# An attention block's output projection moved inside its core, and the last products' operands loaded into freed ring buffers

## The chip, the cores and the metric

One NeuronCore of one Trainium2 chip. The metric is device time in microseconds (us), the median of several executions. Single totals are compared with care, and stages are compared in the traces.

## The reference, cut to what matters

Two attention blocks, A (linear attention) and B (16 query heads over one shared key/value head), each on 2048 tokens of width 448, forward and backward. Only B matters here:

```python
q = (x @ wq).reshape(B, S, 16, 28).transpose(0, 2, 1, 3)     # B_x is (1, 2048, 448)
k, v = x @ wk, x @ wv                                        # one head of 28
p = softmax(einsum("bhqd,bkd->bhqk", q, k) * 28 ** -0.5)
o = einsum("bhqk,bkd->bhqd", p, v)
out = o.transpose(0, 2, 1, 3).reshape(B, S, 448) @ wo        # "the output projection"
# ... and the gradients of x, wq, wk, wv and wo
```

## The kernel before

After block A come 540 "units" `u`, the core. A unit computes scores and exponentials for a slice of 256 keys, the gradient rows of the unit 16 earlier, and more at longer lags. Eight units are a block (one pair of heads, 256 queries); 64 units are a query block of 256 queries. The order of instructions in the core is the program's, engine by engine (no scheduler moves them). Of the names below, eT holds exponentials and eN their transposes; oTs is a block's output as it is copied out of PSUM, onat the normalised output with tokens on the partitions, on_d its copy in DRAM, and oTq (new in the change) the transpose of onat that the output projection reads. gwo, gwq, gwk and gwv are gradients of weights, dx that of x, dq that of the queries.

```python
psS = tile_pool(name="psS", bufs=3, PSUM)    # "sps": scores and small transposes
psD = tile_pool(name="psD", bufs=2, PSUM)    # "dps"
oq, dv_acc, dk_acc = ...                     # one PSUM bank each: all 8 banks are taken
pe_, pn_, pd_ = ...                          # rings eT (10 buffers), eN (11), dsT (4)
...
for u in range(NU + 28):                     # NU = 512
    if u == 14 or u % 64 == 0 and 0 < u < NU:
        # qX: 16 loads of 64 KB on the SP queue; first read at unit u + 28
    # scores -> sps, exp on ScalarE -> eT; at odd u: eN <- DMA transpose of eT (SP queue)
    # gradient rows -> dps; VectorE and ScalarE + GpSimd -> dsT
    e = u - 9
    if e >= 0 and e % 8 == 0 and e // 8 < NB:
        # two transposes of oTs into an sps buffer; VectorE normalises them into onat
        if pair == 7:                        # end of a query block: u % 64 == 1
            nc.sync.dma_start(on_d[...], onat)          # 256 KB to DRAM
    # dk_acc, oq and dv_acc matmuls
    if 0 <= v < NU and v % 8 == 7:           # v = u - 1, so u % 8 == 0
        nc.vector.tensor_copy(out=oTs[v // 8], in_=oq[0:64, 0:256])
# ---- [cut] the tail: new pools, everything loaded here
nc.sync.dma_start(onat_B, on_d)              # 2 MB
load_nat(gb, grad_out); load_nat(xb, B_x)    # 4 x 448 KB each
for g in range(4):
    nc.sync.dma_start_transpose(oT[g], on_d[:, g * P:(g + 1) * P])
for g in range(4):
    nc.sync.dma_start_transpose(dqn[:, :, ...], qT_B[g])
# gwo = onat_B^T gb (64 matmuls); then 16 x (dx: 5 matmuls; output projection: 4 matmuls);
# then gwq, gwk and gwv (128 matmuls)
```

## Time and profile before

| | before |
|---|---|
| median of executions | 1183.8 us |
| span of the profiled execution | 1180.5 us |
| core, from unit 9 to unit 513 | 265.65 to 1074.81 us: 809.2 us |
| from unit 513 to the end | 105.7 us |

The marks "unit 9" and "unit 513" are starts of the two transposes of oTs in those units, in the timeline of TensorE.

The page of the profile: busy tenths of TensorE (PE) and ScalarE (ACT) and the granted clock (PEclk: the share of TensorE's full clock that the chip let through) in 40 slices of 29.5 us, then the chain of waits by line. In later views PEld is TensorE's loading of weights, DVE is VectorE, POOL is GpSimd, and SPq is the queue from which SyncE issues DMAs.

```profile
PE   7999997989999999999999999999999999999778
...
ACT  3453112457999999999999999999999999996112
...
PEclk9999998989999999999999999999999999999889
...
PE dk_acc L590 16%; ACT eT L657 10%; PE oq L590 10%; ACT cp L654 9%; PE sps L590 6%; PE dps L590 5%; PE dv_acc L590 2%; PE pgen L79 2%; PE sps L713 1%; PE pacc L79 1%; SPq L87 1%; SPq L800 1%; DMA out_dram<-osb 1%; ACT eT L647 0%; DMA eN<-eT 0%
```

Both engines are full through the middle, and the chain runs over both: neither alone is the limit. The view by windows gives the length of a window in us and the busy us of each engine (with its count of instructions), for one query block of the core, then for the core's last units and for the tail.

```profile
core 0: us, PE busy (x) PEld busy (x) DVE busy (x) ACT busy (x) POOL busy (x), PEclk, DMA share, GB/s
...
678.50:780.74 102.24, 99.03 (x1696) 36.58 (x1697) 92.19 (x169) 99.88 (x201) 80.90 (x89) 1.00 1.12 181
1074.81:1097.00 22.19, 21.82 (x300) 7.65 (x304) 21.37 (x37) 9.57 (x17) 18.70 (x19) 1.00 0.20 36
1097.00:1180.49 83.49, 66.31 (x416) 32.40 (x411) 12.29 (x22) 17.06 (x35) 3.16 (x3) 0.89 0.72 186
```

A query block takes 102.24 us (every one of them after the first), of which TensorE is busy 99.0 and ScalarE 99.9. The tail from 1097 us is another world: 66 of 83 us on TensorE, at a mean clock of 0.89. What stops it there is in TensorE's timeline of the tail (start, duration, and in brackets the idle time before and what ended it):

```profile
1107.75 13.77 PE L79 MATMUL pacc<-gb_24570,onat_B 128*128 128x448 bf16 x64 [3.62 <-DMA gb_24570<-in_grad_out_dram]
...
1127.04 0.55 PE L79 MATMUL pgen<-wo_24572,oT_24568 128*128 128x448 bf16 x2 [1.93 <-DMA oT_24568<-on_d]
...
1138.35 1.65 PE L79 MATMUL pgen<-wqT_24573,R_63 128*128 128x448 bf16 x4 [3.33 <-ACT osb L840]
```

Loads issued only at 1097 us are waited for, then the transposes oT, then a copy of ScalarE that had itself waited for an output buffer.

The DMA queue of SP around the start of a query block (start, time from the first issue's start to the last one's end, what):

```profile
667.32 8.81 SPq L636 DMA_DIRECT2D qX<-qn_d  x16
676.24 1.96 SPq L660 DMA_TRANSPOSE eN<-eT  x1
678.30 0.94 SPq L687 DMA_DIRECT2D on_d<-onat  x1
679.34 22.30 SPq L660 DMA_TRANSPOSE eN<-eT  x8
```

The 16 qX loads hold the queue for nearly 9 us. One eN transpose follows at 676.24, and on_d's store only at 678.30. TensorE in the same stretch, at the end of unit 8 of that query block:

```profile
677.35 0.29 PE L590 MATMUL oq<-eT,R_65 128*32 128x256 bf16 x2
...
677.68 0.28 PE L590 MATMUL sps<-R_63,R_65 32*128 32x256 bf16 x2
```

Unit 8's oq matmuls are issued by 677.6 and unit 9 begins at 677.68, before on_d's store has even been issued.

### The profile page before, as it was taken

The numbers are of one execution on the slowest core, as the hardware profiler recorded it, in microseconds if no ns is written. First come the engines' busy times: TensorE is split into PE (matmuls) and PEld (weight loads), VectorE is DVE, ScalarE is ACT, GpSimd is POOL, SyncE is SP. The second block draws the span as 40 slices with busy tenths as digits, with TensorE's granted clock in tenths as the row PEclk, the third lists the DMA queues.
The fourth block names the chain that finished last, engine by engine and source line by source line (L and its number), as shares of the span: only waits on it lengthen the run. The fifth ranks groups of instructions, "written<-read, shape, count | busy, mean of one in ns | idle before, by whom it ended". The sixth has DMA issues, their size and how long they took to land.

```text
span 1180.5 us, 38425 instructions
## 1 busy us (share of the span) xinstructions
PE 1108.6 (94%) x15388; PEld 449.4 (38%) x15388; DVE 880.2 (75%) x1655; ACT 906.4 (77%) x1802; POOL 699.8 (59%) x832
## 2 busy tenths in 40 slices
PE   7999997989999999999999999999999999999778
PEld 4555543333333333333333333333333333333334
DVE  7886400336899998899899899899899989989202
ACT  3453112457999999999999999999999999996112
POOL 9000150004787787777777778778777778778200
PEclk9999998989999999999999999999999999999889
DMA  9779797069999999999899999999989999995883
GB/s 258 127 129 185 155 197 167 17 139 174 189 187 174 194 187 169 182 191 184 162 190 182 166 191 176 184 177 186 191 160 182 183 186 174 185 183 95 251 171 104
DMA packets 684514, 203.16 MB, mean 172 GB/s; under 512 B 651056, under 2 KB 679472, under 8 KB 684336
## 3 DMA queue, kind: packets, MB, share of 16 engines
q1 hardware_dynamic: 672592, 189.60, 93.3%
q10 hardware_dynamic: 10464, 7.57, 2.4%
q0 software_dynamic: 1280, 3.55, 1.0%
q8 instruction: 120, 1.97, 0.6%
q14 instruction: 58, 0.48, 0.1%
HBM read 23.09 MB, written 15.03 MB: 32 GB/s over the span
## 4 chain that ended last, share of the span: by engine, by line
PE 44%; ACT 19%; issue 7%; SPq 3%; DMA 2%; DVE 0%; ACTq 0%; POOL 0%; DVEq 0%
PE dk_acc L590 16%; ACT eT L657 10%; PE oq L590 10%; ACT cp L654 9%; PE sps L590 6%; PE dps L590 5%; PE dv_acc L590 2%; PE pgen L79 2%; PE sps L713 1%; PE pacc L79 1%; SPq L87 1%; SPq L800 1%; DMA out_dram<-osb 1%; ACT eT L647 0%; DMA eN<-eT 0%
## 5 line engine op out<-in xcount | busy, mean ns | idle before, releaser
L655 POOL TENSOR_TENSOR dsT<-cp,eT 128x512 bf16<-128x512 bf16 x512 | 590.7, 1154 | 178.1 <-ACT cp L654 140.0
L652 DVE TENSOR_TENSOR dsT<-dps,eT 128x512 bf16<-128x512 f32 x512 | 348.6, 681 | 57.8 <-PE dps L590 33.9
L774 DVE STREAM_TRANSPOSE dsx<-dsT 128x512 f32<-128x512 f32 x512 | 358.2, 700 | 1.0
L647 ACT ACTIVATE eT<-sps 128x512 bf16<-128x512 f32 x512 | 307.6, 601 | 32.0 <-PE dps L590 18.4
L590 PEld LDWEIGHTS <-R_65 32*128 32x128 bf16 (+1 forms) x8192 | 173.3, 92 | 405.2 <-issue 359.2
L654 ACT ACTIVATE cp<-dps 128x512 bf16<-128x512 f32 x512 | 305.4, 597 | 10.2 <-PE dps L590 10.1
L657 ACT ACTIVATE eT<-sps 128x512 bf16<-128x512 f32 x512 | 311.9, 609 | 0.0
L590 PE MATMUL dk_acc<-dsx,qX 32*32 32x512 bf16 x4096 | 289.5, 377 | 0.0
L590 PE MATMUL dps<-doT,R_65 32*128 32x256 bf16 x2048 | 261.7, 272 | 8.1 <-DVE R_64 L761 1.1
L590 PE MATMUL sps<-R_63,R_65 32*128 32x256 bf16 x2048 | 249.7, 277 | 6.2 <-ACT eT L647 2.0
L590 PE MATMUL oq<-eT,R_65 128*32 128x256 bf16 x2048 | 214.5, 278 | 0.6 <-issue 0.2
L590 PE MATMUL oq<-dsT,R_65 128*32 128x256 bf16 x2048 | 203.2, 278 | 0.3 <-ACT R_63 L768 0.2
L590 PEld LDWEIGHTS <-qX 32*32 32x32 bf16 x4096 | 69.9, 89 | 93.1 <-issue 52.0
L590 PE MATMUL dv_acc<-eN,don 128*32 128x512 bf16 x1024 | 85.9, 381 | 0.2 <-DMA eN<-eT 0.2
L521 DVE TENSOR_TENSOR osb<-R_65 32x512 bf16<-32x512 bf16 x4 | 1.7, 413 | 73.1 <-ACT R_65 L518 73.1
L380 POOL MEMSET ga<- 64x448 bf16 x2 | 0.9, 468 | 90.9 <-PE agen L337 71.4
L553 POOL MEMSET R_65<- 128x16 bf16 x1 | 0.2, 172 | 69.6 <-DVE R_65 L552 69.6
L765 DVE COPY oTs<-oq 64x256 f32<-64x256 f32 x64 | 26.6, 416 | 19.1 <-PE oq L590 19.1
L685 POOL TENSOR_TENSOR don<-R_64,rl 128x128 bf16<-128x128 bf16 x64 | 25.7, 402 | 20.9 <-DVE rl L677 20.9
L590 PEld LDWEIGHTS <-don 128*32 128x32 bf16 x1024 | 34.6, 97 | 1.1 <-issue 0.9
L79 PEld LDWEIGHTS <-R_64 128*128 128x128 bf16 x256 | 23.7, 100 | 27.7 <-issue 9.9
L79 PE MATMUL agen<-R_65,R_64 128*128 128x448 bf16 x128 | 29.5, 360 | 3.2 <-DVE pk L227 1.9
(219 smaller groups left out, 965.0 us busy)
## 6 DMA issues: line engine op xcount, KB each, us to landing
qX<-qn_d SPq DMA_DIRECT2D x128, 64.0 KB
out_dram<-osb ACTq DMA_DIRECT2D x60, 112.0 KB
eN<-eT SPq DMA_TRANSPOSE x256
qn_d<-dsx SPq DMA_DIRECT2D x1, 2048.0 KB
on_d<-onat SPq DMA_DIRECT2D x8, 256.0 KB
onat_B<-on_d SPq DMA_DIRECT2D x1, 2048.0 KB
xa<-in_A_x_dram SPq DMA_DIRECT2D x8, 224.0 KB
ga<-in_grad_out_dram SPq DMA_DIRECT2D x4, 448.0 KB
```

The source lines that it names most:

```text
L79: nc.tensor.matmul(out_ap, lhsT=lhsT, rhs=rhs, start=start, stop=stop, tile_position=(0, 0))
L87: eng.dma_start(dst[:, i * NS // n:(i + 1) * NS // n, 0:cols], x2d[i * w:(i + 1) * w, :].rearrange("(t p) d -> p t d", p=P))
L590: nc.tensor.matmul(out, lhsT=lhsT, rhs=rhs, start=start, stop=stop, tile_position=pos, skip_group_check=True)
L647: nc.scalar.activation(out=et[:, u % 2, 0, :], in_=sp[0][:, :], func=ACT.Exp, scale=scale)
L652: nc.vector.tensor_tensor(out=dst[:, 0, :], in0=dp[0][:, :], in1=ew[:, w % 2, 0, :], op=ALU.mult)
L654: nc.scalar.activation(out=cp[:, :], in_=dp[1][:, :], func=ACT.Copy)
L655: nc.gpsimd.tensor_tensor(out=dst[:, 1, :], in0=cp[:, :], in1=ew[:, w % 2, 1, :], op=ALU.mult)
L657: nc.scalar.activation(out=et[:, u % 2, 1, :], in_=sp[1][:, :], func=ACT.Exp, scale=scale)
L685: nc.gpsimd.tensor_tensor(out=dn[:], in0=dnv, in1=r_[:].to_broadcast([P, 2, 2, 32]), op=ALU.mult)
L713: nc.tensor.transpose(tp2[r:r + 64, qb * P:(qb + 1) * P], don[b][:, qb, :, :].rearrange("p h c -> p (h c)"), identB[:, :], tile_position=( ...
L765: nc.vector.tensor_copy(out=oTs[v // 8][:, :], in_=oq[0:64, 0:256])
L774: nc.vector.transpose(out=dsx[b][:, tp, :, :, :].rearrange("p h t c -> p (h t c)").bitcast(F32), in_=dsT[y][:, :, :].rearrange("p h c -> p ...
```

## The change

Its intent: take the output projection out of the tail and do it inside the core, one query block behind; and load the operands of the last products during the core's last units, into ring buffers that these units no longer need, so that the tail starts without waiting. The tail is also put in another order. The diff, cut to its core:

```diff
+        def out_proj(i):
+            ps = psS.tile([P, 512], F32, name="sps")
+            for c in range(4):
+                mm(ps[:, 0:D], oTq[i // 2][:, 4 * (i % 2) + c, :], wo[:, c, :], start=(c == 0), stop=(c == 3))
+            ot = flat(R3)[:, 5120:5120 + D]
+            nc.vector.tensor_copy(out=ot, in_=ps[:, 0:D])
+            nc.sync.dma_start(out0[i * P:(i + 1) * P, D:2 * D], ot)
+        def post_load(k):      # [cut] gb and onat rows and wqT into eT buffers, xb into eN buffers
+        def gwo(n0, n1):       # [cut] the gwo matmuls n0 to n1
 ... in the loop, after the oq, dk_acc and dv_acc matmuls of a unit:
+                if 512 <= u < 530 and u % 2 == 0:
+                    post_load((u - 512) // 2)
+                if u == 530:
+                    # [cut] dqn's four transposes, into a dsx buffer
+                if u >= 530:
+                    gwo(6 * (u - 530), min(64, 6 * (u - 529)))
+                if u % 64 == 1 and u > 1:
+                    q_ = u // 64 - 1
+                    oTq[q_] = pp_.tile([P, 8, P], BF16, name="oTq", bufs=1)
+                    nc.sync.dma_start_transpose(oTq[q_], onat[q_] ...)
+                if u % 64 in (8, 16) and u > 64:
+                    out_proj(2 * (u // 64 - 1) + u % 64 // 8 - 1)
+
                 if 0 <= v < NU and v % 8 == 7:
                     # the oTs copy on VectorE
 ... the tail:
-    # [cut] its pools, loads, oT transposes and the output projection
+    # [cut] rest of gwo, then gwq, gwk and gwv, and dx last, in sps, dps and dsT buffers
```

More of the change, by code (lines that the diff above doesn't have):

```diff
@@ L582 @@
         pm_ = cs_.enter_context(tc.tile_pool(name="csm", bufs=2, side="right"))
+        pp_ = cs_.enter_context(tc.tile_pool(name="cout", bufs=2, side="right"))
         oq = psA.tile([P, 512], F32, name="oq")
@@ L623 @@
         make_identity(nc, identF[:])
+        wo = pp_.tile([P, 4, D], BF16, name="wo", bufs=1)
+        nc.sync.dma_start(wo[:, :, :], wo_d[:, 0:D].rearrange("(g p) c -> p g c", p=P))
+        oTq = {}
+        def out_proj(i):
[5 more added lines that the diff above has]
+            nc.sync.dma_start(out0[i * P:(i + 1) * P, D:2 * D], ot)
@@ new lines, in by_tokens @@
+        def by_tokens(t):
+            return t.rearrange("p (t d) -> p t d", d=512)
+        post = {"gb": [], "on": [], "xb": []}
+        def post_load(k):
+            if k == 0:
+                mix = pq_.tile([P, 4, 2, 512], BF16, name="qX").rearrange("p a b c -> p (a b c)")
+                post["dkvT"], post["dkvn"], post["wkvT"] = mix[:, 0:2048], mix[:, 2048:3072], mix[:, 3072:3072 + D]
+                nc.gpsimd.memset(post["wkvT"][64:128, :], 0.0)
+                nc.gpsimd.memset(post["dkvT"][64:128, :], 0.0)
+                nc.sync.dma_start(post["wkvT"][0:64, :], wkvT_d[:, :])
+            i = k // 2
+            rows = slice(i * 512, (i + 1) * 512)
+            if k == 8:
+                t = pe_.tile([P, 2, 2, 512], BF16, name="eT").rearrange("p a b c -> p (a b c)")
+                post["wqT"] = t[:, 0:4 * D].rearrange("p (g c) -> p g c", c=D)
+                nc.sync.dma_start(post["wqT"], wqT_d[:, :].rearrange("(g p) c -> p g c", p=P))
+            elif k % 2 == 0:
+                t = by_tokens(pe_.tile([P, 2, 2, 512], BF16, name="eT").rearrange("p a b c -> p (a b c)"))
+                nc.sync.dma_start(t[:, :, 0:D], go2[rows, D:2 * D].rearrange("(t p) d -> p t d", p=P))
+                post["gb"] += [t[:, j, :] for j in range(4)]
+                t = by_tokens(pn_.tile([P, 16, P], BF16, name="eN").rearrange("p a b -> p (a b)"))
+                nc.gpsimd.memset(t[:, :, D:512], 0.0)
+                nc.sync.dma_start(t[:, :, 0:D], Bx2[rows, :].rearrange("(t p) d -> p t d", p=P))
+                post["xb"] += [t[:, j, :] for j in range(4)]
+            else:
+                n = 4 if i < 3 else 2
+                t = by_tokens(pe_.tile([P, 2, 2, 512], BF16, name="eT").rearrange("p a b c -> p (a b c)"))
+                nc.sync.dma_start(t[:, 0:n, :], on_d[i * 512:i * 512 + n * P, :].rearrange("(t p) d -> p t d", p=P))
+                post["on"] += [t[:, j, :] for j in range(n)]
+                if i == 3:
+                    post["on"] += [onat[7][:, j, :] for j in range(2)]
@@ new lines, in gwo @@
+        def gwo(n0, n1):
+            for n in range(n0, n1):
+                g_, st = divmod(n, NS)
+                if st == 0:
+                    post["acc"] = psS.tile([P, 512], F32, name="sps")
+                al = post["acc"]
+                mm(al[:, 0:D], post["on"][st][:, g_ * P:(g_ + 1) * P], post["gb"][st][:, 0:D], start=(st == 0),
+                   stop=(st == NS - 1))
+                if st == NS - 1:
+                    sb = pd_.tile([P, 2, 512], BF16, name="dsT")[:, 0, 0:D]
+                    nc.scalar.activation(out=sb, in_=al[:, 0:D], func=ACT.Copy)
+                    for j in range(4):
+                        h = 4 * g_ + j
+                        nc.sync.dma_start(out_8[h * DH:(h + 1) * DH, :], sb[32 * j + 1:32 * j + 1 + DH, :])
@@ L761 @@
                     nc.vector.tensor_copy(out=do_nat[:, v, :], in_=ps[:, :])
+                if 512 <= u < 530 and u % 2 == 0:
+                    post_load((u - 512) // 2)
+                if u == 530:
+                    dqn = px_.tile([P, 8, 2, 2, 256], BF16, name="dsx").rearrange("p a b c d -> p (a b c d)").rearrange(
+                        "p (t d) -> p t d", d=512)
+                    for g_ in range(4):
+                        nc.sync.dma_start_transpose(dqn[:, :, g_ * P:(g_ + 1) * P], qT_B[g_])
+                if u >= 530:
[3 more added lines that the diff above has]
+                    oTq[q_] = pp_.tile([P, 8, P], BF16, name="oTq", bufs=1)
+                    nc.sync.dma_start_transpose(oTq[q_][:, :, :], onat[q_][:, :, :].rearrange("p q c -> p (q c)"))
+                if u % 64 in (8, 16) and u > 64:
+                    out_proj(2 * (u // 64 - 1) + u % 64 // 8 - 1)
                 if 0 <= v < NU and v % 8 == 7:
@@ L776, with gen, sbuf @@
                         in_=dsT[y][:, :, :].rearrange("p h c -> p (h c)").bitcast(F32))
-    with psc, ExitStack() as bs:
-        t4 = bs.enter_context(tc.tile_pool(name="post", bufs=1, side="right"))
-        bwk = bs.enter_context(tc.tile_pool(name="pwk", bufs=3, side="right"))
-        onat_B = t4.tile([P, NS, 512], BF16, name="onat_B")
-        oT = [t4.tile([P, S], BF16, name=f"oT{g}") for g in range(4)]
-        gb = t4.tile([P, NS, D], BF16, name="gb2")
-        xb = t4.tile([P, NS, 512], BF16, name="xb2")
-        wo = t4.tile([P, 4, D], BF16, name="wo2")
-        wqT = t4.tile([P, 4, D], BF16, name="wqT2")
-        wkvT = t4.tile([P, D], BF16, name="wkvT2")
-        dkvT = t4.tile([P, S], BF16, name="dkvT")
-        dqn = t4.tile([P, NS, 512], BF16, name="dqn")
-        dkvn = t4.tile([P, NS, 64], BF16, name="dkvn")
-        nc.sync.dma_start(onat_B[:, :, :], on_d[:, :].rearrange("(t p) c -> p t c", p=P))
-        load_nat(gb, go2[:, D:2 * D], nc.sync)
-        nc.sync.dma_start(wqT[:, :, :], wqT_d[:, :].rearrange("(g p) c -> p g c", p=P))
-        nc.gpsimd.memset(wkvT[:], 0.0)
-        nc.sync.dma_start(wkvT[0:64, :], wkvT_d[:, :])
-        nc.sync.dma_start(wo[:, :, :], wo_d[:, 0:D].rearrange("(g p) c -> p g c", p=P))
-        nc.gpsimd.memset(xb[:, :, D:512], 0.0)
-        load_nat(xb, Bx2, nc.sync)
-        for g in range(4):
-            nc.sync.dma_start_transpose(oT[g][:, :], on_d[:, g * P:(g + 1) * P])
-        nc.gpsimd.memset(dkvT[64:128, :], 0.0)
+        gwo(60, 64)
+        dkvT, wkvT, wqT, xb = post["dkvT"], post["wkvT"], post["wqT"], post["xb"]
+        dkvn = post["dkvn"].rearrange("p (t c) -> p t c", c=64)
+        def gen(i, dt=F32):
+            return [psS, psD][i % 2].tile([P, 512], dt, name=["sps", "dps"][i % 2])
+        def sbuf():
+            return pd_.tile([P, 2, 512], BF16, name="dsT")[:, 0, :]
         for c in range(4):
@@ L806 @@
                                  scale=scale)
-        psc.close()
-        psP = bs.enter_context(tc.tile_pool(name="psP", bufs=4, space=bass.MemoryType.PSUM))
-        def gen(shape, dt=F32):
-            return psP.tile(shape, dt, name="pgen")
-        def accs(w):
-            return [psP.tile([P, w], F32, name="pacc") for _ in range(4)]
-        for g in range(4):
-            nc.sync.dma_start_transpose(dqn[:, :, g * P:(g + 1) * P], qT_B[g])
-        al = accs(D)
-        for g in range(4):
-            for st in range(NS):
-                mm(al[g][:, :], onat_B[:, st, g * P:(g + 1) * P], gb[:, st, :], start=(st == 0), stop=(st == NS - 1))
-            sb = bwk.tile([P, D], BF16, name="gwo_sb")
-            nc.any.tensor_copy(out=sb[:], in_=al[g][:, :])
-            for j in range(4):
-                h = 4 * g + j
-                nc.sync.dma_start(out_8[h * DH:(h + 1) * DH, :], sb[32 * j + 1:32 * j + 1 + DH, :])
+        for c in range(4):
+            r = DC_ROWS[c]
+            al = gen(0)
+            for st in range(NS):
+                mm(al[:, :], xb[st][:, c * P:(c + 1) * P], dqn[:, st, :], start=(st == 0), stop=(st == NS - 1))
+            sb = sbuf()[:, 0:D].rearrange("p (h e) -> p h e", e=DH)
+            nc.vector.tensor_copy(out=sb[0:r], in_=al[0:r, :].rearrange("p (h c) -> p h c", c=32)[:, :, 1:1 + DH])
+            nc.sync.dma_start(out_5[c * P:c * P + r, :].rearrange("r (h e) -> r h e", e=DH), sb[0:r])
         for q4 in range(4):
-            ps = gen([P, 4, P], BF16)
+            ps = gen(1, BF16).rearrange("p (s k) -> p s k", k=P)
             for s in range(4):
@@ L833 @@
             nc.vector.tensor_copy(out=dkvn[:, 4 * q4:4 * q4 + 4, :], in_=ps[:, :, 0:64])
-        for st in range(NS):
-            ps = gen([P, D])
-            for g in range(4):
-                mm(ps[:, :], qT_B[g][:, st * P:(st + 1) * P], wqT[:, g, :], start=(g == 0), stop=False)
-            mm(ps[:, :], dkvT[:, st * P:(st + 1) * P], wkvT[:, :], start=False, stop=True)
-            ot = bwk.tile([P, D], BF16, name="osb")
-            nc.any.tensor_copy(out=ot[:], in_=ps[:, :])
-            nc.sync.dma_start(out4[st * P:(st + 1) * P, :], ot[:])
-            ps = gen([P, D])
-            for g in range(4):
-                mm(ps[:, :], oT[g][:, st * P:(st + 1) * P], wo[:, g, :], start=(g == 0), stop=(g == 3))
-            ot = bwk.tile([P, D], BF16, name="osb")
-            nc.any.tensor_copy(out=ot[:], in_=ps[:, :])
-            nc.scalar.dma_start(out0[st * P:(st + 1) * P, D:2 * D], ot[:])
-        al = accs(512)
         for c in range(4):
             r = DC_ROWS[c]
+            ps = gen(0)
             for st in range(NS):
-                mm(al[c][:, :], xb[:, st, c * P:(c + 1) * P], dqn[:, st, :], start=(st == 0), stop=(st == NS - 1))
-            ps = gen([P, 64])
-            for st in range(NS):
-                mm(ps[:, :], xb[:, st, c * P:(c + 1) * P], dkvn[:, st, :], start=(st == 0), stop=(st == NS - 1))
-            sb = bwk.tile([P, H, DH], BF16, name="gwq_sb")
-            nc.vector.tensor_copy(out=sb[0:r], in_=al[c][0:r, :].rearrange("p (h c) -> p h c", c=32)[:, :, 1:1 + DH])
-            nc.sync.dma_start(out_5[c * P:c * P + r, :].rearrange("r (h e) -> r h e", e=DH), sb[0:r])
-            sk = bwk.tile([P, 2, DH], BF16, name="gwk_sb")
-            nc.scalar.activation(out=sk[0:r], in_=ps[0:r, :].rearrange("p (w c) -> p w c", c=32)[:, :, 1:1 + DH],
+                mm(ps[:, 0:64], xb[st][:, c * P:(c + 1) * P], dkvn[:, st, :], start=(st == 0), stop=(st == NS - 1))
+            sk = sbuf()[:, 0:2 * DH].rearrange("p (w e) -> p w e", e=DH)
+            nc.scalar.activation(out=sk[0:r], in_=ps[0:r, 0:64].rearrange("p (w c) -> p w c", c=32)[:, :, 1:1 + DH],
                                  func=ACT.Copy)
@@ L863 @@
             nc.scalar.dma_start(out_7[c * P:c * P + r, :], sk[0:r, 1, :])
+        for st in range(NS):
+            ps = gen(st)
+            for g in range(4):
+                mm(ps[:, 0:D], qT_B[g][:, st * P:(st + 1) * P], wqT[:, g, :], start=(g == 0), stop=False)
+            mm(ps[:, 0:D], dkvT[:, st * P:(st + 1) * P], wkvT, start=False, stop=True)
+            ot = sbuf()[:, 0:D]
+            if st % 2:
+                nc.vector.tensor_copy(out=ot, in_=ps[:, 0:D])
+            else:
+                nc.scalar.activation(out=ot, in_=ps[:, 0:D], func=ACT.Copy)
+            [nc.scalar, nc.sync][st % 2].dma_start(out4[st * P:(st + 1) * P, :], ot)
+        psc.close()
 _INS = ['A_x', 'A_wqkv', 'A_wo', 'B_x', 'B_wq', 'B_wk', 'B_wv', 'B_wo', 'grad_out']
```

## The prediction

> **What bounds the kernel now.** The attention core (about 283 to 1097 us of a 1180.5 us span) is a tight ring. By windows, TensorE is busy 97% and ScalarE 98% of 500-900 us; in the timeline eight units repeat every 12.78 us; the chain of waits alternates between TensorE (dk_acc 16%, oq 10%) and ScalarE (eT 10%, cp 9%). Neither has over 0.4 us of slack a block. The tail (1097 to 1180.5) is poorly filled: loads issued at 1097, first gwo product at 1107.75, waits for oT transposes at 1124-1129 and output buffers at 1135-1138, three stretches at a granted clock of 0.5.
>
> **Removed from the tail.** 64 output-projection matmuls (12 us), four oT transposes, the wait for gb/onat/xb loads, the buffer waits. What is left after 1097: gwo 12 us with 3 us of dk, gwq 64 x 0.22 = 14.5, transposes and gwk 6, dx 80 x 0.19 = 15, last copy and store 4: about 55 us, with dqn's transposes (12.2 us of issue) hidden under gwo. Tail gain about 28 us.
>
> **Added to the core.** Sixteen out_proj calls, eight oTq transposes.
> 1. Work: 4 matmuls (0.75 us) in a ring with no slack, and a 0.62 us VectorE copy that stands before the oTs copy in VectorE's order; the next unit's transposes and dsT wait behind it. Estimate 1.1 us each, 14 in the core: 15 us, plus 3 us in the drain.
> 2. Waits. In the new order of SP's instructions, oTq's transpose stands behind 16 qX loads, one eN transpose and the on_d store; TensorE meets its first use at unit 8 of the query block. The SP timeline of before shows the qX burst at 667.32-676.1, eN at 676.24, on_d at 678.30-679.24. TensorE passed that point of unit 8 at 677.68, before oTq could even be issued. The eN transpose issued right after on_d landed at 684.9 in the trace; oTq, half its size, would land near 683.7: TensorE stands 6 us. The seven query blocks with a qX burst so give 9.5, 7.6, 5.1, 6.0, 6.0, 4.6, 6.4: about 45 us. The drain's (unit 520) has no burst before it.
> 3. Clock. The Trainium skill ("TensorE: Matmul & The Clock Gate", Part 1) says that an idle window of about 3.4 us puts TensorE to half clock. This trace agrees: after the gap at 179-185 us, and after 1125-1129, the granted clock is 0.5 for 6.8 us and 448-column matmuls stand 0.37 us apart instead of 0.19. Each wait should bring one such stretch, an estimated 2 us each: 14 us.
>
> Core: +74 to 77 us. Net: 1183.85 - 28 + 74 = about 1230.
>
> **Predicted: 1228 us, 8 in 10 between 1200 and 1250. Faster by over 2%: 0.05; within 2%: 0.15; slower by over 2%: 0.80.**
>
> **What would show it.** Right: seven gaps of 4-10 us on TensorE, at the first oTq weight load of a query block, released by the oTq transpose; seven dips of the granted clock; blocks about 1 us longer where out_proj stands; tail near 55 us. Wrong: oTq weight loads with no wait; blocks of unchanged 12.78 us.
>
> **What would make it wrong.** If oTq lands before unit 8, steps 2 and 3 vanish and the result is near 1172. If TensorE's gaps do not bring the half clock, 14 us less. If the slack absorbs the out_proj work, 10 us less. A tail bound by dqn or by stores: 5-10 us more.

## The result, and the profile after

The kernel after takes 1223.8 us (four runs, 1221.0 to 1228.1) against 1183.8 before: the ratio is 1.034, 95% interval 1.030 to 1.038, slower. Ratios here are the mean time of one kernel's fast runs over that of the other's fast runs of the same rounds, so not quite the ratio of the medians.

| | before | after | difference |
|---|---|---|---|
| start to unit 9 | 265.65 | 267.89 | +2.2 |
| unit 9 to unit 513 | 809.16 | 874.52 | +65.4 |
| unit 513 to the end | 105.68 | 81.57 | -24.1 |
| span | 1180.49 | 1223.98 | +43.5 |

The tail gained what it was meant to, and the core lost nearly three times as much. The page of after: the same rows of tenths, now with regular dents in both engines and in the clock, and the group of the projection's matmuls (count, busy us, mean ns, then the idle time of TensorE just before them and what ended it):

```profile
PE   7999988889997998999799979989997999799998
...
ACT  3543212458996998899699969988997999799521
...
PEclk9999989998998999899899989998998999899999
...
L79 PE MATMUL sps<-wo,oTq 128*128 128x448 bf16 x64 | 20.1, 451 | 35.5 <-DMA oTq<-onat 35.5
```

TensorE stood 35.5 us before these 64 matmuls, and the oTq transpose ended it. The view of the chain of waits is no help for this kernel: it reaches back over the last 4% of the span only. The windows of after, in the columns shown before: a query block; TensorE's gap in it; the stretch of half clock behind the gap; one such stretch in the next query block; the core's last units; the tail.

```profile
604.84:716.85 112.01, 102.70 (x1704) 37.26 (x1705) 93.23 (x171) 100.25 (x201) 80.95 (x88) 0.96 1.00 168
708.85:714.10 5.25, 0.01 (x3) 0.00 (x0) 0.00 (x0) 0.71 (x2) 1.15 (x1) 0.93 1.11 226
713.30:720.10 6.80, 5.47 (x50) 1.75 (x54) 3.79 (x9) 2.60 (x6) 1.52 (x2) 0.50 1.23 191
822.50:832.70 10.20, 7.50 (x78) 2.35 (x78) 5.16 (x11) 4.28 (x9) 2.95 (x4) 0.50 1.11 211
1142.41:1170.00 27.59, 25.84 (x305) 8.62 (x306) 23.71 (x41) 9.61 (x18) 21.76 (x25) 0.94 0.99 261
1170.00:1223.98 53.98, 49.00 (x350) 23.69 (x350) 10.02 (x19) 9.92 (x21) 0.00 (x0) 0.98 0.40 92
```

A query block takes 112.0 us (the others after the first 110.4 to 112.6) instead of 102.24, with hardly more work in it. In the second row TensorE does nothing for 5.25 us; the third and fourth have a granted clock of 0.50, for 6.8 and for 10.2 us. The tail's last row shows 49 of 54 us busy at 0.98.

SP's queue in the same place of a query block as before:

```profile
698.29 9.15 SPq L699 DMA_DIRECT2D qX<-qn_d  x16
707.55 2.04 SPq L723 DMA_TRANSPOSE eN<-eT  x1
709.69 0.84 SPq L750 DMA_DIRECT2D on_d<-onat  x1
710.58 1.28 SPq L838 DMA_TRANSPOSE oTq<-onat  x1
```

oTq's transpose is issued at 710.58, behind qX, one eN and on_d. All engines, cut to what follows it:

```profile
708.46 0.29 PE L591 MATMUL oq<-eT,R_65 128*32 128x256 bf16 x2
...
714.13 1.68 PE L79 MATMUL sps<-wo,oTq 128*128 128x448 bf16 x4 [5.28 <-DMA oTq<-onat]
...
715.85 0.62 DVE L635 CAST R_65<-sps 128x448 bf16<-128x448 f32 x1 [7.15 <-PE sps L79]
...
716.39 0.41 DVE L844 COPY oTs<-oq 64x256 f32<-64x256 f32 x1
...
716.85 0.47 PE L731 MATMUL sps<-identF,oTs 64*128 64x64 f32 x2 [0.49 <-DVE oTs L844]
```

TensorE had reached the projection at 708.86 and waits until 714.13, 3.55 us after oTq's issue. Then the four matmuls take 1.68 us where 0.93 is normal (half clock), VectorE copies the projection before it gets to oTs at 716.39, and the transposes of unit 9 wait for that copy. The tail, in TensorE's timeline:

```profile
1186.72 13.98 PE L79 MATMUL sps<-dsx,eN 128*128 128x512 bf16 x62
...
1204.50 0.92 PE L79 MATMUL sps<-eT,R_63 128*128 128x448 bf16 x4 [0.17 <-ACT dsT L892]
```

gwq in 14 us without a break, gwk and gwv in 2.2, dx with 0.17 us of wait: the waits of before are gone.

### The profile page after: what moved, and what is told of

Same layout as the page of the kernel before. It is cut to its first block, busy times and chain, and to the rows that moved or that the text cites. A ratio compares the mean times of both kernels' runs of the same rounds, so it can differ in the third digit from the quotient of the medians.

```text
span 1224.0 us, 38423 instructions
## 1 busy us (share of the span) xinstructions
PE 1120.4 (92%) x15379; PEld 447.0 (37%) x15388; DVE 886.8 (72%) x1669; ACT 901.9 (74%) x1788; POOL 700.0 (57%) x835
## 3 DMA queue, kind: packets, MB, share of 16 engines
q0 software_dynamic: 1280, 3.55, 1.1%
## 5 line engine op out<-in xcount | busy, mean ns | idle before, releaser
L591 PEld LDWEIGHTS <-R_65 32*128 32x128 bf16 (+1 forms) x8192 | 170.8, 93 | 415.6 <-issue 367.2
L591 PE MATMUL dk_acc<-dsx,qX 32*32 32x512 bf16 x4096 | 294.8, 382 | 0.0
L591 PE MATMUL sps<-R_63,R_65 32*128 32x256 bf16 x2048 | 246.9, 282 | 5.5 <-ACT eT L710 2.0
L591 PE MATMUL oq<-eT,R_65 128*32 128x256 bf16 x2048 | 217.7, 283 | 1.8 <-issue 0.5
L591 PE MATMUL oq<-dsT,R_65 128*32 128x256 bf16 x2048 | 208.0, 284 | 1.0 <-POOL dsT L718 0.9
L591 PE MATMUL dv_acc<-eN,don 128*32 128x512 bf16 x1024 | 90.5, 404 | 0.0
L79 PE MATMUL sps<-wo,oTq 128*128 128x448 bf16 x64 | 20.1, 451 | 35.5 <-DMA oTq<-onat 35.5
L635 DVE CAST R_65<-sps 128x448 bf16<-128x448 f32 x16 | 10.0, 625 | 57.3 <-PE sps L79 57.2
L731 PE MATMUL sps<-identF,oTs 64*128 64x64 f32 x128 | 22.4, 258 | 15.3 <-DVE oTs L844 9.1
## 6 DMA issues: line engine op xcount, KB each, us to landing
out_dram<-osb ACTq DMA_DIRECT2D x44, 112.0 KB
```

Of the source, the lines that this page charges most:

```text
L79: nc.tensor.matmul(out_ap, lhsT=lhsT, rhs=rhs, start=start, stop=stop, tile_position=(0, 0))
L591: nc.tensor.matmul(out, lhsT=lhsT, rhs=rhs, start=start, stop=stop, tile_position=pos, skip_group_check=True)
L635: nc.vector.tensor_copy(out=ot, in_=ps[:, 0:D])
L731: nc.tensor.transpose(onp[:, qb, :, :].rearrange("p h c -> p (h c)"), oTs[b][0:64, qb * P:(qb + 1) * P], identF[0:64, 0:64], tile_position ...
```

## The experiments

Nine kernels ran, two of them twice. All results are correct within the usual error unless it is said otherwise. "Pair" is the two projection calls of a query block; its cost is read in the timeline as the excess over 12.78 us of the distances between the oTs transposes of successive blocks around the two calls.

### The projection 16 units later

```diff
-                if u % 64 in (8, 16) and u > 64:
-                    out_proj(2 * (u // 64 - 1) + u % 64 // 8 - 1)
+                d_ = 16 if u < 512 else 0
+                if u > 64 and u % 64 - d_ in (8, 16):
+                    out_proj(2 * (u // 64 - 1) + (u % 64 - d_) // 8 - 1)
```

> out_proj stands 16 units later in the first seven query blocks (units 24 and 32 instead of 8 and 16); nothing else changes. Theory (TensorE waits for the oTq transpose queued behind the qX burst, and comes out of the wait at half clock): no wait on oTq, no stretch at clock 0.5 inside the core, a query block of about 104.5 us instead of 111.6, total 1174 to 1180 us. Rival A (the out_proj work itself in the full ring costs the 65 us: PSUM buffer, VectorE copy ahead of oTs): query block stays above 109 us, total above 1210. Rival B (the DMA traffic added to a nearly full DMA queue slows the ring): likewise above 1205.

Measured: 1173.1 us (1169.3 to 1182.8), ratio to before 0.991 (0.986 to 0.996). That is just under the expected range. No wait on oTq is left, no half clock between units 9 and 513, and a query block takes 104.17 us. Every instruction and every transfer of the change is still there; only fourteen of the projection's calls, with their stores, stand 16 units later. So neither the projection's work (rival A) nor its DMA traffic (rival B) makes up the 65 us; the time at which it asks for oTq does.

### The qX loads later

```diff
-                if u == 14 or u % 64 == 0 and 0 < u < NU:
+                if u == 14 or u % 64 == 12 and 64 < u < NU:
```

> out_proj stays at units 8 and 16; the 16 qX loads are issued at unit 12 of a query block instead of unit 0, so oTq stands behind one eN transpose and the on_d store only. Theory (it is the burst in SP's order): oTq lands before unit 8, waits on oTq fall from 35 us to under 3 us in all, total 1174 to 1182 us. Rival (oTq's own latency behind the eN transposes in the DMA engines is enough to miss unit 8): waits of 2 us or more in each query block, total above 1195.

Measured: 1172.1 us (1169.4 to 1176.2), ratio 0.990 (0.987 to 0.993), just under the expected range; a query block of 104.16 us. SP's queue in this kernel, and the place of the projection:

```profile
676.39 0.54 SPq L750 DMA_DIRECT2D on_d<-onat  x1
676.99 2.17 SPq L838 DMA_TRANSPOSE oTq<-onat  x1
679.26 8.14 SPq L723 DMA_TRANSPOSE eN<-eT  x3
687.49 0.53 SPq L636 DMA_DIRECT2D out_dram<-R  x1
688.12 4.46 SPq L723 DMA_TRANSPOSE eN<-eT  x2
692.63 8.93 SPq L699 DMA_DIRECT2D qX<-qn_d  x16
```

```profile
683.70 0.93 PE L79 MATMUL sps<-wo,oTq 128*128 128x448 bf16 x4
...
684.67 0.62 DVE L635 CAST R<-sps 128x448 bf16<-128x448 f32 x1 [1.07 <-PE sps L79]
...
685.21 0.41 DVE L844 COPY oTs<-oq 64x256 f32<-64x256 f32 x1
...
685.67 0.34 PE L731 MATMUL sps<-identF,oTs 64*128 64x64 f32 x2 [0.71 <-DVE oTs L844]
```

oTq is issued at 676.99 and the projection runs at 683.70 without a wait. So the burst in front of oTq in SP's order was the cause, and the rival, that oTq's own way through the DMA engines is too long for seven units, falls. Another rival is that the burst's traffic, and not its place in SP's order, held oTq up, since this edit moves both. The semaphore events of the traces settle it: the last part of oTq lands 3.6 to 5.2 us after its issue here and 3.4 to 4.3 us in the change, over the seven query blocks. Without the burst oTq does not land sooner after its issue; it is issued sooner.

What is left is 1.92 us for a pair, 0.96 us a call. One call shows 0.93 us of matmuls and then, at 685.67, a wait of 0.71 us for the oTs copy, which VectorE reaches only after the projection's copy; a part of that is caught up again (the block after the pair takes 12.59 us instead of 12.78).

### Keeping TensorE's clock up through the wait

```diff
+            if i % 2 == 0 and i < 14:
+                for n in range(20):
+                    mm(ps[:, 0:D], wo[:, n % 4, 0:P], wo[:, n % 4, :])
             for c in range(4):
                 mm(ps[:, 0:D], oTq[i // 2][:, 4 * (i % 2) + c, :], wo[:, c, :], start=(c == 0), stop=(c == 3))
```

> Twenty matmuls of 128x448 on resident data (3.8 us, their result is overwritten) fill most of the wait before the first out_proj of a query block; the wait itself stays. Theory (the half clock after the wait costs about 2 us a block, 14 us in all): no clock of 0.5 in the core, total 1208 to 1213 us although TensorE executes 140 more matmuls. Rival (the clock costs nothing because ScalarE bounds the ring, all of the 65 us is waits and work): total 1221 or more.

Measured: 1214.1 us (1213.3 to 1217.5), ratio 1.025 (1.023 to 1.027): 9.7 us less than the change, with 140 matmuls more. TensorE around one of the waits, and the query block that follows:

```profile
704.66 3.96 PE L79 MATMUL sps<-wo 128*128 128x448 bf16 x20
709.80 0.93 PE L79 MATMUL sps<-wo,oTq 128*128 128x448 bf16 x4 [1.18 <-DMA oTq<-onat]
```

```profile
711.80:821.70 109.90, 103.65 (x1724) 38.81 (x1724) 92.94 (x171) 100.04 (x201) 80.99 (x88) 1.00 1.03 171
```

The wait for oTq is still there (1.18 us of it remain visible after 3.96 us of dummy work), and the clock stays at 1.00. Five of the seven waits came out warm. The marks then give the price of the half clock. Take a query block's excess over the plain ring, read as for a pair (6.6 to 7.9 us in these five), and subtract the whole time from TensorE's last matmul of the core to the projection's first (4.6 to 5.9 us, dummy matmuls included). What is left is 1.99 to 2.00 us each time: the pair itself, 1.92 us in the qX-later kernel, and 0.07 us by which its first matmul there overlaps the one before. So a wait that stays warm costs its own length and nothing more. In the change's seven query blocks the same subtraction leaves 3.7 to 4.6 us. Less 1.99 each, the half clock costs 1.7 to 2.6 us a wait, 15.3 us in all, which is 0.27 to 0.29 us for each us of half clock after TensorE's restart; the two waits of this kernel that came out cold give about 0.29 as well. The waits themselves were longer here, 38.8 us against 35.5, so that the total fell by 9.7 us only. The expectation was missed: the median lies 1 us over 1208 to 1213, and two waits still brought the half clock.

### The new tail without the projection

oTq and out_proj are taken out; the right half of out_0 is not written.

> The new tail alone: no oTq and no out_proj (the right half of out_0 is not written, wrong on purpose). Theory: query blocks of 102.24 us as before, no waits, tail from unit 513 about 78 us instead of 105.7; total 1154 to 1160 us. Rival (the ring-buffer loads or the new tail cost the core something too): total above 1165.

Measured: 1155.5 us (1151.9 to 1159.2), ratio 0.975 (0.972 to 0.978). The query blocks take 102.24 us; from unit 513 to the end 77.6 us, 28.1 less than before. With the last two projection calls there (the qX-later kernel) it is 80.4. The core takes 809.1 us, as before. So the new tail and its loads cost the core nothing.

### The projection back in the tail

The tail is as changed, the projection stands behind dx; its operands come by four DMA transposes of on_d, issued behind dqn's, into four freed eN buffers.

```diff
+                    oT = [pn_.tile([P, 16, P], BF16, name="eN").rearrange("p a b -> p (a b)") for _ in range(4)]
+                    for g_ in range(4):
+                        nc.sync.dma_start_transpose(oT[g_], on_d[:, g_ * P:(g_ + 1) * P])
```

> The other half of the change alone: the new tail with its loads in freed ring buffers, but the output projection left in the tail, last of all, on operands that four DMA transposes of on_d bring into four freed eN buffers behind dqn's. Theory (the whole gain of the change is the early loads; the projection costs TensorE as much in the core as in the tail, or more): query blocks of 102.24 us, tail about 12.5 us longer than without the projection, total 1166 to 1170 us, under the 1172 of the version with the projection in the core and no wait. Rival (hiding the projection in the core is what gains): total above 1176.

Measured: 1169.8 us, ratio 0.987 (0.984 to 0.990); see the repeat below. From unit 513 to the end 89.5 us, 11.9 more than without the projection. Hiding it in the core isn't what gains: two calls in the last units cost 2.8 us and fourteen in the ring another 13 (in the place they have in the change), more than 12 in the tail.

### Where in the eight-unit pattern the projection stands

```diff
-                if u % 64 in (8, 16) and u > 64:
+                p_ = u // 64 % 8
+                if u > 64 and u % 64 in (8 + p_, 16 + p_):
```

> qX loads at unit 12, and out_proj in each of the first seven query blocks at another place of the eight-unit pattern: query block 1 at units 9 and 17, block 2 at 10 and 18, up to block 7 at 15 and 23 (unit 8 and 16 were measured: 1.92 us for the pair). Theory (the ring has slack only where TensorE stands waiting for ScalarE, in units 1 to 3 of the pattern): pairs at 1 to 3 cost under 1.2 us, pairs at 5 to 7 cost 1.5 us or more. Rival (the cost is the work itself wherever it stands): every pair costs 1.7 to 2.1 us.

Measured (one execution, 1173.2 us), the cost of a pair at offsets 0 (from the qX-later kernel) to 7:

| offset | 0 | 1 | 2 | 3 | 4 | 5 | 6 | 7 |
|---|---|---|---|---|---|---|---|---|
| us a pair | 1.92 | 1.96 | 2.04 | 2.21 | 2.20 | 2.31 | 2.56 | 3.22 |

My theory of slack in units 1 to 3 is wrong: no place hides the work. The rival is right about that, and wrong about it being equal everywhere: it rises towards the end of the pattern. The change's own place was the cheapest. Each offset was tried in one query block only, and from offset 4 on the pair's first call stands at or behind the qX loads, now issued at unit 12; whether they have a part in the rise was not tested.

### The parts of a projection call

One kernel, another variant in each query block. Its output is wrong, which doesn't matter for the time.

> qX loads at unit 12, out_proj at units 8 and 16, and in each query block another part of it (outputs wrong on purpose): q=0 whole; q=1 whole, but its VectorE copy stands behind the oTs copy; q=2 the four matmuls with a copy of one column, no store; q=3 one matmul and the whole copy, no store; q=4 half of the columns, into the unused half of oq's bank instead of an sps buffer; q=5 the copy on ScalarE; q=6 whole without store. Theory (half of the 0.96 us a call is the copy that stands ahead of oTs in VectorE's order): pair costs 1.9 at q=0, under 1.4 at q=1, 0.8 to 1.2 at q=2, 0.8 to 1.4 at q=3, about 1.9 at q=6. Rival (it is TensorE's matmul time alone): 1.5 to 1.9 at q=1 and q=2, under 0.6 at q=3.

Measured (one execution):

| variant | us a pair |
|---|---|
| whole | 1.92 |
| whole, its copy behind the oTs copy | 1.28 |
| four matmuls, a copy of one column | 1.26 |
| one matmul, the whole copy | 0.99 |
| half the columns, into oq's bank | 1.32 |
| copy on ScalarE | 1.47 |
| whole, no store | 1.92 |

A third of the cost is the order of two copies on VectorE; the store costs nothing. The matmuls with almost no copy (1.26) cost as much as all of the call with its copy behind oTs (1.28): in that order the copy seems to be nearly free, and what is left TensorE's time, though no variant ran the matmuls with no copy at all. (Matmuls alone came out above my range of 0.8 to 1.2, below the rival's.)

The half-column variant spoilt a gradient: out_5 had a relative error of 0.154 where other kernels have 0.005. It began an accumulation in oq's bank while oq's own sums, in other columns, were running. The Trainium skill ("PSUM — Partial Sum Buffer", The four PSUM rules) says that the first matmul of a group clears the has_written bits of the whole bank in the quadrants that it writes, so that later matmuls overwrite there. The error agrees with it, in size too. At units 8 and 16 the o sums in that bank have just ended, while the dq sums in its other quadrants are 14 of 16 matmuls in; out_5, the gradient of wq, is made from dq. Two of the 64 blocks were hit so. An estimate from these counts, the root of 2/64 times 14/16, is 0.155.

### The best version, two repeats, and late loads

The first kernel joins the qX loads at unit 12 with the copy behind the oTs copy:

```diff
-                if u % 64 in (8, 16) and u > 64:
-                    out_proj(2 * (u // 64 - 1) + u % 64 // 8 - 1)
                 if 0 <= v < NU and v % 8 == 7:
                     oTs[v // 8] = pm_.tile([64, 256], F32, name="oTs")
                     nc.vector.tensor_copy(out=oTs[v // 8][:, :], in_=oq[0:64, 0:256])
+                if u % 64 in (8, 16) and u > 64:
+                    out_proj(2 * (u // 64 - 1) + u % 64 // 8 - 1)
```

> The version that should beat the others: qX loads at unit 12, out_proj at units 8 and 16, its VectorE copy behind the oTs copy. From the parts run (1.28 us a pair against 1.92): 4.5 us under the version with the copy in front, about 1167 to 1168 us; query blocks of 103.5 us. If the gain of the parts run doesn't add up, 1171 to 1173.

> Repeat of the qX-later kernel, beside the two others on the same chip: 1172 us, ratio to before 0.990.

> Repeat of the projection-in-the-tail kernel: 1169 to 1170 us, ratio 0.987: 1 to 4 us under the qX-later kernel and 1 to 3 us over the copy-behind-oTs kernel. If it isn't under the qX-later kernel, the earlier difference was noise.

Measured on one chip, five rounds each:

| kernel | median us | ratio to before | 95% interval |
|---|---|---|---|
| copy behind oTs, qX later | 1166.3 | 0.985 | 0.9832 to 0.9875 |
| qX later (repeat) | 1172.4 | 0.991 | 0.9883 to 0.9944 |
| projection in the tail (repeat) | 1166.9 | 0.985 | 0.9832 to 0.9875 |

The copy behind oTs and the projection in the tail cannot be told apart, and both are faster than the qX-later kernel (the intervals do not overlap, by a little). The first and the last of the three expectations named slightly longer times (1167 to 1168 and 1169 to 1170 us). Against the kernel before both gain 1.5%, clear of noise but less than 2%. The expected gain of 4.5 us is there: a query block takes 103.52 us and a pair 1.28, and the core from unit 9 to 513 is 4.4 us shorter than in the qX-later kernel. The place of the projection in the best version:

```profile
681.93 0.93 PE L79 MATMUL sps<-wo,oTq 128*128 128x448 bf16 x4
...
682.12 0.42 DVE L841 COPY oTs<-oq 64x256 f32<-64x256 f32 x1 [0.29 <-PE oq L591]
...
682.90 0.62 DVE L635 CAST R<-sps 128x448 bf16<-128x448 f32 x1 [0.36 <-PE sps L79]
...
683.58 0.33 PE L731 MATMUL sps<-identF,oTs 64*128 64x64 f32 x2 [0.39 <-DVE R L635]
```

oTs is copied at 682.12, ahead of the projection's copy at 682.90. The transposes of unit 9 still wait 0.39 us, now for their sps buffer, which the projection's copy frees.

The last kernel is the qX-later one with all loads of the last products issued together:

```diff
-                if 512 <= u < 530 and u % 2 == 0:
-                    post_load((u - 512) // 2)
+                if u == 529:
+                    for k in range(9):
+                        post_load(k)
```

> As the qX-later kernel, but all loads of the last products are issued together at unit 529, about where the old kernel issued them, instead of from unit 512 on. Theory (the early loads hide about 10 us of the old wait from 1097 to 1107.75 and a cold start of TensorE): a wait of 6 to 11 us before the first gwo products or between them, total 1180 to 1186 us. Rival (the tail gains by its order and by the projection's leaving, not by the loads' time): total under 1176.

Measured: 1188.3 us (1187.4 to 1190.7), ratio 1.004 (1.002 to 1.006). This is outside both ranges, above the theory's: the loads' time matters more than I said. TensorE in its tail, then one window of this kernel, then the same window of the qX-later kernel:

```profile
1122.64 1.68 PE L79 MATMUL sps<-eT 128*128 128x448 bf16 x4 [7.86 <-DMA eT<-on_d]
1127.14 1.67 PE L79 MATMUL sps<-eT 128*128 128x448 bf16 x4 [2.82 <-DMA eT<-on_d]
```

```profile
1115.00:1142.00 27.00, 12.99 (x61) 3.57 (x62) 1.48 (x3) 0.74 (x2) 1.39 (x5) 0.56 1.07 279
```

```profile
1115.00:1142.00 27.00, 26.95 (x175) 11.46 (x175) 2.89 (x5) 4.89 (x9) 0.00 (x0) 1.00 0.53 107
```

TensorE waits 14.2 us in four places for rows of on_d, and with bursts of four matmuls between the waits it gets a mean clock of 0.56 in this window. From unit 513 to the end it takes 99.1 us against 80.4: the 18.7 us are 14.2 of waits and about 4.5 that the half clock would explain, which was not tested by itself. So issuing the loads early is worth about 19 us against issuing them all at unit 529. The projection's leaving is worth another 12 less the 2.8 of its two last calls. Together that is 28 where 25.3 was gained from before (105.7 to 80.4), so the split is rough: this kernel's order of loads isn't quite the old tail's.

## Why the prediction was right

The text said 1228 us and slower with a chance of 0.8; 1223.8 was measured. That the two are so close is in part luck: the text's own terms add up to +49 us, of which it took 46 and then rounded down, and the largest was 9.5 us too big. Term by term:

| term | predicted | measured | from |
|---|---|---|---|
| waits for oTq, seven | 45 us | 35.5 us | idle before the projection's matmuls |
| half clock after them | 14 us | 15.3 us | what is left of the seven excesses after the wait and 1.99 us each |
| work of 14 calls in the ring | 15 us | 13.4 us | seven pairs of 1.92 us in the qX-later kernel (whose whole core, 822.06 us against 809.16, is 12.9 longer) |
| two calls in the last units | 3 us | 2.8 us | 80.4 against 77.6 us from unit 513 |
| tail | -28 us | -28.1 us | tail without the projection |

The measured terms add up to 38.9 us, and the spans differ by 43.5. Of the rest, 2.2 us lie before unit 9; 1.2 us lie behind unit 513, where the change and the 16-units-later kernel show a half-clock stretch of 3.4 us and a tail of 81.5 us, and the qX-later kernel neither (80.4); about 1 us is the start of the ring and the 0.07 us of each restart.

- **Waits (step 2) were right in cause, and the term was too big.** The burst of qX loads, not the projection's work or traffic, makes oTq late: two independent edits that only separate the two (the projection later, the loads later) each removed all of the waits. The trace divides the 35.5 us: oTq was issued 0.6 to 2.4 us after TensorE had reached the projection, 10.1 us in all, and was in use 3.4 to 4.4 us after its issue, 25.5 us in all. The mis-sized term is for the most part oTq's landing. I took the landing of a full-size eN transpose and shortened it for the half size (4.4 us after issue in the query block shown); oTq was in use 3.4 to 3.6 us after its issue in six of seven query blocks. In the first two query blocks the issue, too, was less late than in the trace of before: the guesses were 9.5 and 7.6 us, the waits 5.3 and 4.3.
- **Clock (step 3) was right.** The Trainium skill ("TensorE: Matmul & The Clock Gate", Part 1) has half clock after an idle window of about 3.4 us; all seven gaps, 4.3 to 5.9 us, brought it, and the windows show 0.50 for 6.8 or 10.2 us. The forecast of 2 us a wait was near (1.7 to 2.6). One of the two instances that the text gives from the trace of before fits the window less well: between 1125 and 1129 us there is no single gap of that length but one of 1.9 and one of 1.4 us. Filling the gaps gave 9.7 us back.
- **Work (step 1) was right in size**, and in its reason for a third: the copy standing ahead of oTs is worth 0.32 us of 0.96 a call. Moving it was worth 4.4 us in the traces and 6 us in the medians of the last table.
- **The tail was right.** The prediction did not say how the 28 us divide; by the late-loads kernel, most of it hangs on when the loads are issued.
- The sentence about what would make it wrong can be checked as well: "if oTq lands before unit 8 ... near 1172". With the loads out of the way it lands in time, and 1172.1 us was measured.

What stays open: why a half-clock stretch lasts 6.8 us in some places and 10.2 in others. In each of the traces all changes of the clock fall on one grid of 3.41 us (within 2 ns), so these are two steps and three, but what decides the third is not shown. Nor is it shown why two of the waits filled with dummy matmuls came out cold, with visible gaps of 1.75 and 2.51 us, and others, with 1.84 and 1.99, warm.

## What to carry to other kernels

Before work is moved into a full pipeline, look at what stands in front of its operands in the queue that brings them. Here the order of issue decided, and a late operand stopped everything behind it on TensorE for 4.3 to 5.9 us, with a cold clock after it each time. Moving work "into the shadow" gained nothing here, where the engine in the shadow was already 97% busy: most of what gained was the early loading (about 19 of 25 us, by the late-loads kernel), and the projection cost as much inside as in the tail. When two copies on one engine can stand in either order, put the one that the next step of the ring waits for first.

## What the Trainium skill lacked or had wrong

- "TensorE: Matmul & The Clock Gate": it gives half clock after an idle window of 3.4 us, and a warm-up of about 3.4 us. Here half clock lasted 6.8 or 10.2 us after single gaps of 4.3 to 5.9 us; it also came after 4 us of dummy matmuls and a gap of 1.75 us, and it stayed through waits of 2.8 us between bursts of four matmuls (mean clock 0.56 over 27 us in the late-loads kernel). The rule on its page, no gaps over about 3 us, was not strict enough in these places; the page does tell of a kernel in which short idles bring the half clock back, but gives no length for them.
- "DMA: Bandwidth & Descriptors": Issuing engines are not separate DMA queues: it says that the time a sequencer takes to issue a DMA is "usually small relative to the DMA itself". One load of 64 KB took 0.42 us (median) to issue here, but 16 of them in a row held SP's queue for 8.4 to 10.4 us, and an urgent transpose behind them came late by enough to stop TensorE 35.5 us in all. That section doesn't warn of what a burst adds up to.
- "DMA: Bandwidth & Descriptors", Latency and other measured facts: it has a bandwidth for DMA transposes (261 GB/s, at which oTq's 256 KB would be an estimated 1.0 us) but no time from issue to use of a transpose behind other transfers: here TensorE used it 3.4 to 3.6 us after issue in six query blocks and 4.4 us in one.
